# A transformer block on one core: weight splitting moved to the first attention block, key loads by pairs, and a changed planner table

## The chip, the cores and the metric

The kernel runs on one core of a Trainium2 chip. The metric is the device time of one execution in microseconds (us), from its start to its end; smaller is better. The core has five engines that run their own instruction streams in order: TensorE (PE, matrix products; PEld is its weight load), VectorE (DVE), ScalarE (ACT), GpSimd (POOL) and SyncE (SP), which here does nothing but issue DMAs. An instruction that waits holds back everything behind it on its engine.

## The reference

One block: an adaptive layer norm, multi-head attention with 32 heads of width 18 on 2048 tokens of width 576, a second adaptive layer norm, and a two-layer network of width 4608 with SiLU.

```python
mod = (_silu(c) @ w_mod).reshape(c.shape[0], 6, 1, -1)
sa, ca, ga, sb, cb, gb = (mod[:, 0], ..., mod[:, 5])
h = _layernorm(x, axis=-1) * (1 + ca) + sa
x = x + ga * _A_ref(h, A_wqkv, A_wo)     # softmax(q k^T / sqrt(18)) v, then @ wo
h = _layernorm(x, axis=-1) * (1 + cb) + sb
x = x + gb * _B_ref(h, B_w1, B_w2)       # silu(h @ w1) @ w2
```

## The kernel before

**Number format.** To keep precision with TensorE's reduced fp32 format, weights and activations are split into a high and a low part and multiplied in three products (high-high, high-low, low-high). Splitting a weight means a load into `raw`, a copy with rounding on POOL (`CAST`, high part), a subtraction on POOL (low part) and, since the same weights are needed four times, a store of both parts to a scratch tensor (`w1s`, `w2s`, `wos`). The function `weights` does this for the first of the four uses; later uses load the two parts from scratch.

**Staging.** The first part (to about 150 us) makes the first layer norm, the first q, k and v projections and their splits, and starts the scores. Then the attention runs in 4 query blocks of 512 tokens. A block has 8 "quads" of 4 heads, a quad 32 "slots", a slot two score pairs. For each pair TensorE makes two products at once, each on half of its rows: `psa` (scores, `ka` times `qt`, whose maximum DVE takes, `slot_a`) and, 40 slots later in the program (`LEAD`), `psb` (the same scores transposed, `kb` times `qt`, with the maximum subtracted inside the product; ACT takes the exponential into a `pt` buffer, `slot_b`). Then `psv` multiplies `pt` with the values (`pv`, four column groups of the array at once). When a quad is done, ACT copies `psv` to `ov`, DVE transposes and normalises it, and SP copies the heads into `ou` by DMA (`out_b`).

**Filler work.** Between score pairs TensorE is given other work from a list (`Filler`). In block 0 this is the rest of the q/k projections (`psqk`, function `qk_one`, weights by `qk_load`). When that list is empty, `open_mlp` closes the memory pools of the projections and opens the pool `mlp` in their place. In block b+1 the filler is what follows the attention of block b: splitting `ou` into `th` and `tl` (`o_T`), the output projection (`psp`), layer norm, transposes (`h_T`), and the network (`mlp1`, `mlp2`, with the weights `w1t` and `w2t`). The network of the last block runs alone at the end.

**What sets the order.** TensorE's order is written by a planner (`Plan`): a clock with costs in ns for each kind of work, queues for ACT and DVE with a duration for each operation (`TMAX` for a maximum, `TEXP` for an exponential), and rings for the PSUM banks, so that a product is put where its bank should be free. It is a list made at build time; on the chip only semaphores decide when things run. The other engines' orders (ACT, DVE, POOL and SP) come from a list scheduler with a timeline of its own, which may pull an instruction ahead of others if its inputs look ready.

**Lines that the steps touch.** `L690` psa, `L692` its maximum, `L739` psb, `L741` its exponential, `L776` psv, `L780` the copy to ov, `L804` ou from ov, `L872` the copy th from ou, `L664` key loads, `L717` and `L721` the maxima's way through DRAM (mscr) into the rows of `qt`, `L834` raw loads, `L837` and `L838` the split on POOL, `L839` the store of a split weight, `L565` and `L572` ACT's copies of a finished projection, `L588` its store, `L900` the addition of an output to x on POOL.

## Time and profile before

| | |
|---|---|
| median of 3 runs | 2464.64 us (2460.85 to 2469.64) |
| the profiled execution | 2463.14 us, of which 2461.4 us are the span from its first to its last instruction |
| busy in the span | PE 96%, DVE 73%, ACT 61%, POOL 26% |
| granted TensorE clock, mean | 0.981 |
| DMA | 433.01 MB, 176 GB/s in the mean |

Busy times of PE are modelled ends of pipelined products, so 96% does not mean that it works at its peak. A row of the timeline gives start, duration, engine, line, operation, output and inputs, and in brackets how long the engine was idle before and what released it. Rows of the windows view give a stretch in us, then its length, then per engine the busy time and the instruction count in the order PE, PEld, DVE, ACT, POOL, then the granted clock, the share of the 16 DMA engines and GB/s.

### The profile page before, as it was taken

Reading aid. Unit: us, or ns where it says so; the run is one execution under the profiler, and the core shown is the slowest. Engines: PE = TensorE matmul, PEld = TensorE weight load, DVE = VectorE, ACT = ScalarE, POOL = GpSimd, SP = SyncE. Lnnn points to the kernel's source line nnn. Section 1 sums busy time; section 2 is a strip of 40 time slices with the busy share of each in tenths; the row PEclk is TensorE's granted clock in tenths of the full one; section 3 lists DMA queues with packets and bytes.
Section 4 is the critical chain, followed back from the end, with each engine's and each line's share of the span. In section 5 each row is a group of like instructions: output and inputs, shape, how many; then the busy total and the mean of one; then the engine's idle time right before and its main releaser. Section 6 shows DMA issues by size and latency. Waiting matters only on the chain.

```text
span 2461.4 us, 52349 instructions
## 1 busy us (share of the span) xinstructions
PE 2359.8 (96%) x19952; PEld 1585.1 (64%) x19952; DVE 1789.9 (73%) x3110; ACT 1497.0 (61%) x2736; POOL 628.6 (26%) x763
## 2 busy tenths in 40 slices
PE   6989999998999999999999999998999999989999
PEld 4864444433556666766667667775666766678998
DVE  7868888876777888777888888887888788234333
ACT  4227777765566777666677677775677677732121
POOL 5201111122565666554211111112211111110000
PEclk9999999999899999999999999999999999999999
DMA  7744445454466676664545554453655454426563
GB/s 242 250 154 151 147 150 161 143 160 146 144 202 195 227 227 209 206 211 164 182 147 202 171 178 157 164 179 117 217 176 162 155 197 165 133 90 241 183 214 119
DMA packets 201458, 433.01 MB, mean 176 GB/s; under 512 B 31354, under 2 KB 67610, under 8 KB 201210
## 3 DMA queue, kind: packets, MB, share of 16 engines
q1 hardware_dynamic: 196618, 427.37, 52.4%
q8 instruction: 160, 2.62, 0.5%
q10 hardware_dynamic: 4592, 2.29, 0.4%
q14 instruction: 88, 0.72, 0.1%
HBM read 338.53 MB, written 86.33 MB: 173 GB/s over the span
## 4 chain that ended last, share of the span: by engine, by line
PE 82%; DMA 6%; DVE 5%; POOL 2%; ACT 2%; issue 2%; SPq 1%; ACTq 0%; POOLq 0%; DVEq 0%
PE ps L480 25%; PE psv L776 17%; PE psa L690 12%; PE ps L474 10%; PE psb L739 8%; PE psqk L561 4%; DVE mx L692 2%; PE psv L480 2%; PE psp L480 1%; DMA raw<-in_w 1%; DMA mscr<-mt 1%; PE psv L1238 1%; PE psqk L1238 1%; PE psqk L480 1%; PE psp L474 1%
## 5 line engine op out<-in xcount | busy, mean ns | idle before, releaser
L692 DVE TENSOR_REDUCE mx<-psa 128x1 f32<-128x512 f32 x2048 | 1333.0, 684 | 334.5 <-PE psb L739 199.6
L741 ACT ACTIVATE pt<-psb 128x512 f32<-128x512 f32 x2048 | 1150.5, 598 | 511.0 <-PE psb L739 350.0
L739 PE MATMUL psb<-qt,kb 56*128 56x512 f32 x2048 | 772.6, 427 | 39.2 <-ACT pt L741 22.0
L690 PE MATMUL psa<-ka,qt 54*128 54x512 f32 x2016 | 739.4, 420 | 10.9 <-DVE mx L692 8.7
L690 PEld LDWEIGHTS psa<-ka,qt 54*128 54x128 f32 x2016 | 344.1, 188 | 316.3 <-DVE mx L692 213.4
L776 PE MATMUL psv<-pt,vt 128*32 128x512 f32 x4096 | 521.4, 608 | 2.0 <-ACT ov L780 2.0
L480 PE MATMUL ps<-w2t,g 64*128 64x288 f32 x4992 | 418.4, 296 | 0.2
L739 PEld LDWEIGHTS psb<-qt,kb 56*128 56x128 f32 x2048 | 357.4, 187 | 90.3 <-ACT pt L741 61.0
L480 PEld LDWEIGHTS ps<-w2t,g 64*128 64x128 f32 x4992 | 390.7, 188 | 32.7 <-DVE mx L692 13.4
L480 PE MATMUL ps<-hh,w1t 64*128 64x512 f32 x2160 | 384.7, 395 | 1.7 <-DVE x L896 1.6
L480 PEld LDWEIGHTS ps<-hh,w1t 64*128 64x128 f32 x2160 | 216.4, 186 | 60.6 <-DVE mx L692 10.9
L1016 POOL TENSOR_TENSOR g<-etmp,g 128x512 fp32r<-128x512 f32 x108 | 138.8, 1305 | 397.6 <-ACT g L1015 318.0
L776 PEld LDWEIGHTS psv<-pt,vt 128*32 128x32 f32 x4096 | 98.5, 109 | 211.7 <-issue 203.4
L900 POOL TENSOR_TENSOR x<-x,gt 128x288 f32<-128x288 f32 x116 | 92.7, 801 | 427.0 <-ACT gt L899 426.9
L480 PE MATMUL ps<-hl,w1t 64*128 64x512 f32 x864 | 181.1, 392 | 0.0
L896 DVE TENSOR_TENSOR x<-ps,x 128x288 f32<-128x288 f32 x184 | 83.8, 456 | 122.0 <-PE ps L474 76.6
L474 PE MATMUL ps<-w2t,g 128*128 128x288 f32 x960 | 132.9, 299 | 7.4 <-ACT g L1015 5.9
L474 PEld LDWEIGHTS ps<-w2t,g 128*128 128x128 f32 x960 | 130.6, 191 | 9.9 <-ACT g L1015 6.3
L1012 ACT ACTIVATE eq<-ps 128x512 f32<-128x512 f32 x36 | 21.5, 598 | 146.4 <-PE ps L474 146.4
L474 PE MATMUL ps<-hh,w1t 128*128 128x512 f32 x360 | 106.9, 390 | 0.5 <-DVE hh L415 0.5
L480 PEld LDWEIGHTS ps<-hl,w1t 64*128 64x128 f32 x864 | 90.5, 187 | 16.5
L1013 DVE SCALAR_TENSOR_TENSOR etmp<-etmp 128x512 f32<-128x512 f32 x108 | 78.1, 759 | 22.1 <-ACT etmp L1012 21.3
(141 smaller groups left out, 2025.4 us busy)
## 6 DMA issues: line engine op xcount, KB each, us to landing
w1t<-w1s SPq DMA_DIRECT2D x108, 640.0 KB
w2t<-w2s SPq DMA_DIRECT2D x108, 576.0 KB
kb<-kscr SPq DMA_DIRECT2D x512, 108.0 KB
ka<-kscr SPq DMA_DIRECT2D x504, 108.0 KB
w1s<-w1t SPq DMA_DIRECT2D x36, 640.0 KB
w2s<-w2t SPq DMA_DIRECT2D x36, 576.0 KB
vt<-vscr SPq DMA_DIRECT2D x32, 608.0 KB
qt<-qscr SPq DMA_DIRECT2D x128, 108.0 KB
```

Source lines behind the costliest of these rows:

```text
L474: mm(self.ps[late], lhsT=lhsT, rhs=rhs, start=(i == 0), stop=(i == self.n - 1))
L480: done = mm(self.ps[g], lhsT=lhsT[rows], rhs=rhs[rows], start=(s == 0), stop=(s == 2 * self.n - 1))
L561: mm(qk_ps[0], lhsT=w[b][:, kt, :], rhs=(hTl if a else hTh)[:, kt, n * 512:(n + 1) * 512], start=(i == 0), stop=(i == 13))
L690: mm(ps, lhsT=t["q"][64 * j:64 * j + 54, hp, stt * P:(stt + 1) * P], rhs=t["a" if ("a", kc, hp) in t else "b", kc, hp][64 * j:64 * j + 54, ...
L692: return lambda: nc.vector.tensor_reduce(t["mx"][:, 2 * j + hp, stt, kc:kc + 1], ps, axis=AX.X, op=ALU.max)
L739: mm(ps, lhsT=t["b", kt // 4, hp][64 * e:64 * e + 56, kt % 4 * P:(kt % 4 + 1) * P], rhs=t["q"][64 * e:64 * e + 56, hp, :], start=True, sto ...
L741: nc.scalar.activation(t["P"][kt, hp][:, e, :], ps, AF.Exp, scale=SCALE)
L776: mm(t["ps"][32 * h:32 * h + 32, :], lhsT=t["v"][:, c0:c0 + 32], rhs=t["P"][kt, h // 2][:, h % 2, :], start=(kt == 0), stop=(kt == NKT - 1 ...
L896: nc.vector.tensor_add(c["x1"][j][:, hs], ps, c["x1"][j][:, hs])
L900: nc.gpsimd.tensor_add(c["x1"][j][:, hs], c["x1"][j][:, hs], t)
L1013: nc.vector.scalar_tensor_tensor(t, t, 1.0, u, op0=ALU.add, op1=ALU.mult)
L1016: (nc.vector if last else nc.gpsimd).tensor_tensor(g[:, 1, :], t, f(g[:, 0, :]), op=ALU.subtract)
```

## The change

- The first-layer weights (36 tiles) and the output weights (5) are split during block 0's projections, in a staging pool `early` (tiles `we`, 2 buffers; `raw`, 3 buffers), and stored to scratch. Block 0's own network then loads them from scratch. The second-layer weights are still split where they were.
- Key loads are asked for one pair of heads at a time, at four points of every 8 slots: slot 1 (second pair of the next `ka`), slot 5 (first pair of the one after), slots 2 and 4 (the two pairs of the next `kb`). Before, all four loads of a ring were asked for at slot 0.
- The copies `th` from `ou` get a dependency on the score product that TensorE's order has last at that point (`after_pe`).
- The q/k weights are loaded over SP instead of ACT's queue, and the load is asked for earlier than the split.
- `pt` has 7 buffers until `open_mlp` and 10 from then on (3 are taken from the `mlp` pool, and are the next to be used); the planner's durations are shorter (`TMAX` 690 to 605, `TEXP` 600 to 495) with a latency added behind each operation (`TLAT`); `LP`, a pause that the filler's pace counts ahead of block 0's transposes, goes from 8000 to 2000.

```diff
-LP = 8000
-PB = 10
+LP = 2000
+PB = 7, 10
-TMAX, TEXP = 690, 600
+TMAX, TEXP = 605, 495
+TLAT = {"A": 100, "V": 85}
...
-                done(s + dur)
+                done(s + dur + TLAT[e])
...
+    def after_pe(ins):
+        if state["pe"] is not None:
+            tc.add_manual_dep(ins.ins, state["pe"].ins.name, SYNC, reason="its turn by the plan")
...
     def qk_load(which, m, i):
-        raw = qk_raw.pop(i)() if i in qk_raw else raw_load(qk_src(which, m), KT * P, nc.scalar)
+        if i not in qk_raw:
+            raw = raw_load(qk_src(which, m), KT * P, nc.sync)
+            qk_raw[i] = lambda: raw
+
+    def qk_split(i):
+        raw = qk_raw.pop(i)()
         hi = hi_part(raw)
...
                     if n == pairs[0][0] and p == 0 and i + 1 < len(steps):
                         load(i + 1)
+                    if n == pairs[0][1] and p == 0 and i + 1 < len(steps):
+                        split(i + 1)
+                    if p % 2 == 1 and splits:
+                        fill.add(0, splits.pop(0))
...
+    def early(src, scr, gate=None):
+        weights(mp["e"].tile([P, 2, 640], F32R, tag="w", name="we", bufs=2)[:, :, :src.shape[1]], src, scr, True, gate)
...
+    splits = [lambda i=i: early(w1[i], w1s[i]) for i in range(NFT)] + [lambda kt=kt: early(wo[:, kt, :], wos[kt], ga) for kt in range(KT)]
...
-        if (s + KLD) % 8 == 0 and 32 <= s + KLD < 32 * NQ:
-            load_k("a", (s + KLD) // 8)
+        n, w = divmod(s, 8)
+        if w == 1:
+            if s == LEAD + 1:
+                load_k("a", n + 1, 0)
+            load_k("a", n + 1, 1)
+        elif w == 5:
+            load_k("a", n + 2, 0)
...
-            if s % 8 == 0 and s and s + 8 < 32 * NQ:
-                load_k("b", s // 8 + 1)
+            if s >= 8 and s % 8 in (2, 4):
+                load_k("b", s // 8 + 1, s % 8 // 2 - 1)
...
-            t["P"][kt, hp] = pts[s % PB]
+            t["P"][kt, hp] = pts[0]
+            pts.append(pts.pop(0))
...
+        pts[:0] = [mp["p"].tile([P, 2, QB], F32, name=f"pt{i}") for i in range(*PB)]
...
-            weights(w, wo[:, kt, :], wos[kt], b == 0, ga)
+            weights(w, None, wos[kt], False)
...
-            nc.scalar.activation(hi[:n], src[:n], AF.Copy)
+            after_pe(nc.scalar.activation(hi[:n], src[:n], AF.Copy))
...
-            weights(c["w1", i], w1[i], w1s[i], b == 0)
+            weights(c["w1", i], None, w1s[i], False)
```

**How the orders move.** Three places matter below. The first is ACT at the end of block 0's projections. The last projection is copied out (`qkhl`, `qt`), then exponentials (`pt`) follow. Before:

```order
L572 ACTIVATE qkhl<-psqk 128x512 [waits DMAHW6_49,DMAHW5_49,PE_49]
L565 ACTIVATE qt<-psqk 128x512 [waits Pool_49]
L741 ACTIVATE pt_2089<-psb 128x512 [waits PE_49]
L741 ACTIVATE pt_2090<-psb 128x512 [waits PE_49] x2
L741 ACTIVATE pt_2091<-psb 128x512 [waits PE_49] x2
L872 ACTIVATE th<-ou 128x512 [waits DMAHW2_49,DMAHW4_49,DMAHW1_49,DMAHW6_49,DMAHW0_49,Pool_49]
```

After, at the same place (`pt_6971` is the first of the three buffers in the `mlp` pool):

```order
L580 ACTIVATE qkhl<-psqk 128x512 [waits DMAHW4_49,DMAHW0_49,PE_49]
L573 ACTIVATE qt<-psqk 128x512 [waits Pool_49]
L779 ACTIVATE pt_6971<-psb 128x512 [waits DMAHW2_49,DMAHW6_49,DMAHW0_49,DMAHW7_49,PE_49,Pool_49]
L779 ACTIVATE pt_6971<-psb 128x512 [waits PE_49]
L779 ACTIVATE pt_6972<-psb 128x512 [waits PE_49] x2
```

The first three copies `th` have left this place. The wait for POOL and for DMAs, which goes with the first tile that is written in the new pool (its memory was that of the projections' tiles, whose last stores have to land), now stands on an exponential, directly behind the projection's copies.

The second place is ACT at the end of a block's last quad, where `ov` is copied and the last two copies `th` wait for its way through DVE and the DMAs `ou<-ov`. Here the end of block 0, before:

```order
L780 ACTIVATE ov<-psv_6339 128x512
L741 ACTIVATE pt_2096<-psb 128x512 x2
L741 ACTIVATE pt_2097<-psb 128x512 x2
L872 ACTIVATE th<-ou 128x512
L741 ACTIVATE pt_2098<-psb 128x512 x2
L741 ACTIVATE pt_2089<-psb 128x512
L872 ACTIVATE th<-ou 64x512
```

After:

```order
L818 ACTIVATE ov<-psv_6772 128x512
L779 ACTIVATE pt_2098<-psb 128x512 x2
L896 ACTIVATE th<-ou 128x512 x3
L779 ACTIVATE pt_2092<-psb 128x512 x2
L779 ACTIVATE pt_6971<-psb 128x512 x2
L779 ACTIVATE pt_6972<-psb 128x512 x2
L779 ACTIVATE pt_6973<-psb 128x512 x2
L779 ACTIVATE pt_2093<-psb 128x512 x2
L896 ACTIVATE th<-ou 128x512
L896 ACTIVATE th<-ou 64x512
```

Between `ov` and the copy that needs it stand 12 exponentials and three other copies, where 4 exponentials stood. At the ends of blocks 1 and 2 there are 12 exponentials now where 6 and 2 stood.

The third place is SP in block 0's second quad. Before, a stretch of it:

```order
L664 DMA ka_80<-kscr 54x512 x2
L664 DMA kb_86<-kscr 54x512 x2
L664 DMA ka_81<-kscr 54x512 x2
L664 DMA kb_87<-kscr 54x512 x2
L586 DMA kscr<-qkhl 128x512
L588 DMA kscr<-qkhl 128x2x512
```

After, a stretch with the same key loads:

```order
L696 DMA ka_80<-kscr 54x512
L649 DMA w1s<-we 128x1280
L696 DMA ka_80<-kscr 54x512
L644 DMA raw<-in_w 128x320 x2
L649 DMA w1s<-we 128x1280
L644 DMA raw<-in_w 128x320 x2
L649 DMA w1s<-we 128x1280
L644 DMA raw<-in_w 128x320
L696 DMA kb_86<-kscr 54x512 x2
```

The scheduler does not spread the 36 first-layer splits over block 0's projections: of their stores 16 stand between the first and the second DMA `mscr<-mt` (one per quad), 15 between the second and the third, 5 between the third and the fourth, and none later. DMAs on SP in these three intervals are 92, 98 and 66, where they were 40, 52 and 51.

Counted over the whole order, TensorE changes between its three kinds of work (products on half of the rows, on the full array, and by column groups for the values) 908 times before and 857 times after: 449 and 431 times in block 0, 38 and 29 in the first quad of block 1. In that quad it now has 72 half-row products of the first layer where it had 36.

77 lines of the change are left out of this document (38 added, 39 removed).

## The prediction

> **What bounds the kernel now.** I read the page's first part, then the windows by stage: first attention block (154 to 514 us), the turn to block 1 (to 600), block 1 to its last quad (to 1062), two stretches of eight quads (to 1580 and 2098), and the network alone.
>
> ```profile
> PE 2359.8 (96%) x19952; PEld 1585.1 (64%) x19952; DVE 1789.9 (73%) x3110; ACT 1497.0 (61%) x2736; POOL 628.6 (26%) x763
> 154.00:514.00 360.00, 357.83 (x2207) 156.00 (x2204) 301.40 (x512) 262.50 (x508) 38.90 (x31) 1.00 0.47 148
> 514.00:600.00 86.00, 71.32 (x373) 27.62 (x371) 59.40 (x101) 52.50 (x98) 26.70 (x36) 0.89 0.56 178
> 600.00:1062.00 462.00, 444.13 (x4118) 299.94 (x4115) 360.77 (x605) 303.89 (x551) 277.45 (x384) 0.97 0.60 196
> 1062.00:1580.00 518.00, 507.45 (x4891) 348.63 (x4890) 411.92 (x698) 357.43 (x649) 123.66 (x140) 0.99 0.53 177
> 1580.00:2098.00 518.00, 508.47 (x4955) 349.70 (x4954) 416.12 (x708) 359.74 (x655) 91.29 (x91) 0.99 0.50 167
> ```
>
> TensorE is the bound. It is full in the first window (357.8 of 360) and idles by 15 us in the second and 18 in the third, against 10 to 11 in the later two; there, too, the clock is lowest and POOL busiest. From 514 to 1062 are 548 us for eight quads that later take 518: that is where something can be won. So I looked in the timeline at what ended TensorE's idle times of more than 1 us. Most are ACT's waits at the copies `th`:
>
> ```profile
>   DMA ou<-ov: 14.5, 4
>   DMA qscr<-qkhl: 4.3, 1
> 543.52 1.15 ACT L872 ACTIVATE th<-ou 128x512 fp32r<-128x512 f32 x2 [4.35 <-DMA qscr<-qkhl]
> 545.21 0.79 PE L739 MATMUL psb<-qt,kb 56*128 56x512 f32 x1 [4.78 <-ACT pt L741]
> 596.32 0.63 ACT L872 ACTIVATE th<-ou 128x512 fp32r<-128x512 f32 x1 [5.65 <-DMA ou<-ov]
> 597.49 1.28 PE L739 MATMUL psb<-qt,kb 56*128 56x512 f32 x2 [5.03 <-DMA ka<-kscr]
> 1151.77 0.63 ACT L872 ACTIVATE th<-ou 128x512 fp32r<-128x512 f32 x1 [3.47 <-DMA ou<-ov]
> 1674.87 0.63 ACT L872 ACTIVATE th<-ou 128x512 fp32r<-128x512 f32 x1 [4.27 <-DMA ou<-ov]
> 595.00:602.00 7.00, 4.51 (x16) 1.80 (x16) 1.99 (x3) 3.77 (x8) 1.27 (x1) 0.51 0.17 53
> 1151.00:1158.00 7.00, 5.07 (x25) 2.87 (x27) 2.33 (x4) 3.79 (x7) 1.27 (x1) 0.53 0.29 93
> 1677.00:1684.00 7.00, 5.64 (x29) 3.02 (x29) 3.86 (x6) 3.76 (x7) 0.00 (x0) 0.51 0.03 12
> ```
>
> ACT stands at a copy, exponentials queue behind it, banks stay taken, `psb` stops. Each stop is followed by about 7 us at half the clock.
>
> **The change part by part.** The sum is made against the profiled execution, 2463.1 us; the median of the runs is 1.5 us above it. A difference under 0.3% (7.4 us) is what a measurement here cannot tell from none.
>
> *Copies in TensorE's order.* At the block ends they now stand behind 12 exponentials, where they stood behind 4, 6 and 2. At 0.8 to 0.95 us an exponential (a quad's 64 in 51 to 62 us) these and the three other copies take over 11 us; `ov` to `th` took 8 to 9 (in the timeline around the rows above). So the 14.5 us of waits should go: **+13**, 12 to 14.5. The three slow-clock stretches cost up to 3.5 us each, but part of that time is idle anyway: **+6**, 0 to 10.
>
> *The first wait stays.* At 543.52 the copy waited for the projections' last store. By the order that wait now stands on the first exponential in a new buffer, and no exponential is ahead of it.
>
> ```profile
> 535.44 0.59 ACT L565 ACTIVATE qt<-psqk 128x512 f32<-128x512 f32 x1
> 536.11 1.28 POOL L566 TENSOR_TENSOR qkhl<-qt,qkhl 128x512 fp32r<-128x512 f32 x1 [11.97 <-ACT qt L565]
> 537.41 0.39 SPq L588 DMA_DIRECT2D qscr<-qkhl  x1
> ```
>
> From the end of `qt` (536.0) to the release (543.5) are 7.5 us, in which before five exponentials ran. ACT stands 7.5 instead of 4.35: **-3**, -5 to 0. This part of the stall moves and does not go.
>
> *First-layer splits out of block 1.* They leave POOL 98 us lighter there, of 277.
>
> ```profile
> L838 POOL TENSOR_TENSOR w1t<-raw,w1t 128x320 fp32r<-128x320 f32 x72 | 63.4, 892 | 0.3
> L837 POOL CAST w1t<-raw 128x320 fp32r<-128x320 f32 x72 | 34.4, 487 | 74.4 <-DMA raw<-in_w 45.6 <-DMA kb<-kscr 9.1 <-PE psa L690 7.5
>   DMA raw<-in_w: 121.5, 77
> 638.30 0.46 DVE L906 BATCH_NORM_STATS2 st<-x 128x6 f32<-128x288 f32 x1 [4.47 <-POOL x L900]
> 639.85 0.79 PE L690 MATMUL psa<-ka,qt 54*128 54x512 f32 x1 [2.77 <-DVE mx L692]
> 641.00:657.00 16.00, 15.12 (x54) 6.57 (x53) 11.54 (x24) 8.75 (x15) 10.89 (x15) 0.52 0.69 235
> ```
>
> What POOL's time costs is its order: it stood 121.5 us at loads not yet landed, with the additions to x behind. At 638 that stopped DVE, then TensorE for 2.8 us, and 16 us at half clock followed, worth up to 8. Second-layer splits stay and keep some such waits: **+12**, 3 to 16.
>
> *The burst.* The order puts 31 of the 36 splits into two quads of block 0.
>
> ```profile
> L717 SPq DMA_DIRECT2D mscr<-mt x32: 342/343/1072, 153.9 to 2098.0; - x32
> 258.83 0.34 SPq L717 DMA_DIRECT2D mscr<-mt  x1
> w1s<-w1t SPq DMA_DIRECT2D x36, 640.0 KB
> raw<-in_w SPq DMA_DIRECT2D x72, 160.0 KB
> 200.00:250.00 50.00, 50.00 (x304) 21.54 (x296) 41.63 (x71) 36.84 (x71) 5.37 (x4) 1.00 0.46 148
> 2220.00:2230.00 10.00, 7.10 (x39) 4.94 (x38) 7.08 (x14) 3.64 (x5) 2.93 (x4) 1.00 1.01 401
> 80.00:100.00 20.00, 20.00 (x192) 17.38 (x193) 16.72 (x37) 2.66 (x7) 1.54 (x1) 1.00 1.01 316
> ```
>
> These quads last from 153.9 to 258.8, 104.9 us. POOL has room: 31 x 2 x (0.487 + 0.892) = 85.5 us. The DMA engines have less: a split moves 640 + 2 x 160 KB = 0.98 MB, 31 of them 30.5 MB; at 148 GB/s the quads' own traffic is 15.5 MB; 46.0 MB in 104.9 us are 439 GB/s. With all engines busy (share 1.01) the trace shows 401 and 316. SP issues in order, so key loads stand behind loads and stores that wait, and fall behind with them. At 401 GB/s the two quads take 114.7 us, at 316 145.6, which is 10 or 41 late. What hides a delay is the key loads' lead: a `kb` load for a pair is now asked for 5 or 6 slots ahead (8 and 9 before), 8 to 10 us; a store of 512 KB landed 6 us after its issue (537.4 to 543.5), a key load is smaller. I take 4 us as cover: a loss of 6 to 37. The splits' packets are large like those of the 401 row, so I stay in the lower half: **-15**. The Trainium skill, "DMA: Bandwidth & Descriptors" (Specifications), gives about 358 GB/s as one core's share of HBM and 435 as the fabric's ceiling; by the first the loss would be about 20 and the sum 5 us worse, by the second about none. The 401 row speaks against the first as a hard limit.
>
> *Fewer changes of kind on TensorE.* Counted over the order, 51 fewer.
>
> ```profile
> 580.44 0.50 PE L739 MATMUL psb<-qt,kb 56*128 56x512 f32 x1
> 581.87 0.50 PE L690 MATMUL psa<-ka,qt 54*128 54x512 f32 x1
> 582.21 0.39 PE L690 MATMUL psa<-ka,qt 54*128 54x512 f32 x1
> 582.44 0.39 PE L690 MATMUL psa<-ka,qt 54*128 54x512 f32 x1
> 670.68 1.93 PE L776 MATMUL psv<-pt,vt 128*32 128x512 f32 x16
> 672.53 0.50 PE L690 MATMUL psa<-ka,qt 54*128 54x512 f32 x1
> ```
>
> Two value tiles take 1.85 us (670.68 to 672.53), one 0.93. From the `psb` at 580.44 over one value tile to the `psa` at 581.87 are 1.43 us; less the tile and a product's 0.23 (582.21 to 582.44), 0.27 remain, and 0.11 more before the next `psa` (0.34 for 0.23). A pair of changes costs 0.27 to 0.38, 51 changes 7 to 10. Some fall in the burst: **+8**, 5 to 10.
>
> *Earlier network work.* 36 more half-row products in block 1's first quad, where TensorE had idle time, at half of 0.23 us each: **+4**, 0 to 8. With `LP` gone the transposes `h_T` come a few slots behind the last `psp`, and their layer norm may not be ready: **-2**, -4 to 0, once.
>
> *Key loads by pairs.* Both rings' loads keep their number. The waits `psb` had for `qt<-mscr` may shrink when SP is blocked less; a shorter `kb` lead may add some:
>
> ```profile
>   PE psb L739: 9.7, 4
> ```
>
> **+1**, -4 to +10.
>
> *At nothing.* The q/k weights' 7 loads on SP are asked for one step ahead, and a step of two units is some 30 us in this stage. 7 `pt` buffers: the order has as many runs of value products in block 0 (127) as before, so the cover is the planner's own check. Shorter planner durations cost nothing by themselves; what they do is in the order above.
>
> Sum: 13 + 6 - 3 + 12 - 15 + 8 + 4 - 2 + 1 = **24 us faster**, 2439; with the median's 1.5 us, **2440.5**.
>
> **The rivals.** *The burst starves the scores* (slower). Without its term the sum is 39 faster. It cancels that when the two quads are 43 us late, 148 us, that is at 311 GB/s; below 296 the kernel is slower by more than the bound. At 270 GB/s they take 170 us, 61 lost: 2463 - 39 + 61 = 2485, 2487 as a median. For it: mixed loads and stores have no row above 316 that lasts 20 us, and a core that waits keeps its clock low. Against: the two rows quoted, and that POOL's and SP's waits also make the demand drop.
>
> *The waits move.* The copies' 19 us come back as the longer first wait, as waits of `h_T`, and as ACT's three copies in a row; 24 - 19 = 5 faster, 2459 (2460). For it: the first wait moved just so. Against: 12 exponentials are more than the trace's 8 to 9 us.
>
> *The burst costs nothing and block 1 becomes like the others*: 548 against 518 us is 30, with the copies at blocks 1 and 2 and the order 47: 2416 (2418).
>
> **How the numbers follow.** Forecast 0.62, between 2418 and 2456; the waits move 0.12; the starved scores 0.20; the larger gain 0.06. Range 2412 to 2474: from the terms' good ends, a little beyond the larger gain, into the lower part of the starved case, leaving out its worse half (0.1) and a tenth for the rest. Faster by over 0.3%: 0.62 + 0.06 = 0.68; the waits move is the same, 0.12; slower 0.20.
>
> **What would show it.** Right: `th` no longer waits for `ou<-ov` before 2100; one exponential waits about 7.5 us for `qscr<-qkhl` near 540; POOL busy about 180 in block 1's eight quads instead of 277, and no half-clock stretch of 16 us near 640; DMA share near 1 from 155 to 260 with the third `mscr<-mt` later than 258.8 by some 15 us. Wrong: the third `mscr<-mt` later by over 40 us, with `ka` and `kb` loads ending TensorE's waits there; or not later at all, and then the time is near 2425; or waits of exponentials behind `th` as long as before.

## The result, and the profile after

| | median, us | ratio to the kernel before (95% interval) |
|---|---|---|
| before | 2464.56 (2460.85 to 2469.64, 4 runs) | |
| changed | 2493.38 (2491.18 to 2497.5, 4 runs) | 1.0117 (1.0095 to 1.014) |

The kernel is 29 us slower; 24 us faster was forecast, and the range ended at 2474. All windows, waits and intervals below come from the one profiled execution of each kernel; times and ratios are of all its runs. The windows by stage of the changed kernel say where (columns as before: PE, PEld, DVE, ACT, POOL busy, granted clock, DMA share, GB/s):

```profile
154.00:206.00 52.00, 40.76 (x218) 16.69 (x218) 35.00 (x57) 28.05 (x54) 27.30 (x44) 0.91 0.81 263
206.00:259.00 53.00, 33.35 (x142) 13.97 (x142) 19.98 (x33) 18.43 (x34) 31.30 (x48) 0.70 0.79 264
259.00:312.00 53.00, 41.06 (x205) 18.04 (x203) 26.29 (x45) 24.04 (x46) 26.69 (x39) 0.81 0.82 279
312.00:365.00 53.00, 40.88 (x225) 16.64 (x225) 33.30 (x53) 28.33 (x54) 19.65 (x26) 0.87 0.77 251
365.00:514.00 149.00, 148.29 (x901) 62.76 (x903) 128.12 (x221) 113.48 (x223) 38.37 (x44) 1.00 0.58 178
577.00:1097.00 520.00, 496.27 (x4401) 328.54 (x4401) 406.61 (x690) 345.23 (x640) 200.32 (x257) 0.96 0.55 181
```

Block 0's first quads, where TensorE was full before, are now its emptiest place: 156 of 211 us, at a clock of 0.70 to 0.91. From 365 us on TensorE is full again. The DMA engines are busy, but at 0.77 to 0.82 and not at 1.

One mark makes the kernels comparable: the DMA `mscr<-mt`, issued once a quad when its maxima are complete. Its start times on SP are numbered from 0 here, and the intervals are differences of these times, in us:

| | transfer 0 at | 0 to 1 | 1 to 2 | 2 to 3 | three together | 8 to 15 |
|---|---|---|---|---|---|---|
| before | 153.9 | 53.3 | 51.6 | 49.4 | 154.3 | 484.3 |
| changed | 144.4 | 90.5 | 85.6 | 55.5 | 231.5 | 455.9 |

So 9.6 us are won ahead of the first transfer, 77 lost in three intervals, and 28 won back in block 1; the other 11 are won in small parts, 4 in intervals 3 to 8 and 7 behind transfer 15. The largest single stop is in SP's order. Timeline rows of the changed kernel, SP first, then TensorE:

```profile
222.09 3.35 SPq L644 DMA_DIRECT2D raw<-in_w  x2
225.93 0.33 SPq L649 DMA_DIRECT2D w1s<-we  x1
226.34 0.38 SPq L644 DMA_DIRECT2D raw<-in_w  x1
226.82 0.32 SPq L696 DMA_DIRECT2D kb<-kscr  x1
227.19 0.95 SPq L594 DMA_DIRECT2D kscr<-qkhl  x1
...
231.97 0.54 SPq L596 DMA_DIRECT2D kscr<-qkhl  x1
...
234.84 0.38 SPq L754 DMA_DIRECT2D mscr<-mt  x1
239.15 1.28 SPq L758 DMA_DIRECT2D qt<-mscr  x2
224.12 0.50 PE L727 MATMUL psa<-ka,qt 54*128 54x512 f32 x1
242.03 0.89 PE L777 MATMUL psb<-qt,kb 56*128 56x512 f32 x2 [17.41 <-DMA qt<-mscr]
```

TensorE has finished the quad's last `psa` at 224.6, and DVE its last maximum at 225.4. The maxima leave only at 234.84, because raw loads, split stores and projection stores stand ahead of them on SP, and TensorE stands until 242. What SP waited for from 154 to 365 us (waits of the DMA queue; total, times, longest):

```profile
SPq L644 <- POOL we L648: 31.2, 20, 2.6
SPq L644 <- DMA raw<-in_w: 10.7, 9, 2.7
SPq L649 <- POOL we L648: 9.0, 16, 2.0
```

Raw loads wait until POOL's subtraction has freed one of three buffers (20 times), stores until that subtraction is done (16 times): 40 us of waits for POOL, with the key loads and the maxima behind.

### The profile page after: what moved, and what is told of

Its sections match the earlier page's. It is cut to its first block, busy times and chain, and to the rows that moved or that the text cites. A ratio compares the mean times of both kernels' runs of the same rounds, so it can differ in the third digit from the quotient of the medians.

```text
span 2489.4 us, 52376 instructions
## 1 busy us (share of the span) xinstructions
PE 2357.8 (95%) x19952; PEld 1615.3 (65%) x19952; DVE 1781.6 (72%) x3110; ACT 1482.3 (60%) x2736; POOL 627.6 (25%) x763
## 2 busy tenths in 40 slices
DMA packets 208003, 459.56 MB, mean 185 GB/s; under 512 B 32010, under 2 KB 68266, under 8 KB 207754
## 4 chain that ended last, share of the span: by engine, by line
PE 82%; DMA 6%; DVE 5%; ACT 3%; POOL 2%; issue 2%; SPq 1%; ACTq 0%; POOLq 0%; DVEq 0%
PE ps L483 25%; PE psv L814 17%; PE psa L727 12%; PE ps L477 10%; PE psb L777 9%; PE psqk L569 3%; DMA raw<-in_w 3%; DVE mx L729 2%; PE psv L483 2%; PE psp L483 1%; DMA kb<-kscr 1%; PE psv L1262 1%; PE psqk L483 1%; ACT pt L779 1%; PE psqk L1262 1%
## 5 line engine op out<-in xcount | busy, mean ns | idle before, releaser
L779 ACT ACTIVATE pt<-psb 128x512 f32<-128x512 f32 x2048 | 1131.4, 598 | 554.2 <-PE psb L777 372.0
L777 PE MATMUL psb<-qt,kb 56*128 56x512 f32 x2048 | 762.3, 432 | 71.5 <-ACT pt L779 22.2
L727 PE MATMUL psa<-ka,qt 54*128 54x512 f32 x2016 | 703.8, 421 | 10.3 <-DVE mx L729 8.8
L777 PEld LDWEIGHTS psb<-qt,kb 56*128 56x128 f32 x2048 | 357.1, 188 | 122.2 <-ACT pt L779 57.5
L483 PE MATMUL ps<-w2t,g 64*128 64x288 f32 x4992 | 408.5, 293 | 0.2
L483 PEld LDWEIGHTS ps<-w2t,g 64*128 64x128 f32 x4992 | 382.6, 186 | 30.7 <-DVE mx L729 7.5
L483 PE MATMUL ps<-hh,w1t 64*128 64x512 f32 x2160 | 397.9, 393 | 2.5 <-DVE x L920 1.5
L483 PEld LDWEIGHTS ps<-hh,w1t 64*128 64x128 f32 x2160 | 247.3, 185 | 37.9 <-DVE mx L729 7.5
L483 PE MATMUL ps<-hl,w1t 64*128 64x512 f32 x864 | 200.2, 391 | 0.0
L483 PEld LDWEIGHTS ps<-hl,w1t 64*128 64x128 f32 x864 | 107.3, 186 | 9.3
```

The source lines that it names most:

```text
L483: done = mm(self.ps[g], lhsT=lhsT[rows], rhs=rhs[rows], start=(s == 0), stop=(s == 2 * self.n - 1))
L727: mm(ps, lhsT=t["q"][64 * j:64 * j + 54, hp, stt * P:(stt + 1) * P], rhs=t["a" if ("a", kc, hp) in t else "b", kc, hp][64 * j:64 * j + 54, ...
L777: state["pe"] = mm(ps, lhsT=t["b", kt // 4, hp][64 * e:64 * e + 56, kt % 4 * P:(kt % 4 + 1) * P], rhs=t["q"][64 * e:64 * e + 56, hp, :], s ...
L779: nc.scalar.activation(t["P"][kt, hp][:, e, :], ps, AF.Exp, scale=SCALE)
```

## The experiments

**Which part costs, which part gains.**

*Splits' DMAs on POOL's queue* (`weights`, while the early pool is open):

```diff
-            nc.sync.dma_start(raw, src[:, cs])
+            q.dma_start(raw, src[:, cs])      # q = nc.gpsimd for the early splits
-        nc.sync.dma_start(f(scr), f(w))
+        q.dma_start(f(scr), f(w))
```

> The changed kernel with one edit: the early splits' loads and stores are issued from POOL's own queue and no longer from SP's; their bytes, their tiles and their place in POOL's order stay. The changed kernel is at 2493 us and loses 73 us against the kernel before between the first and the eighth transfer of the maxima (231.5 us for the first three intervals instead of 154.3). Theory 'queue' (each split's loads wait on SP until POOL has freed one of three buffers, and the key loads stand behind them): nothing of the splits stands in SP's order any more, the three intervals fall to 155 to 175 us, the time to 2420 to 2440. Theory 'bandwidth' (30 MB more than the DMA engines can move beside the key loads): the same bytes in the same stretch, so the three intervals stay over 210 us and the time over 2475. In between (some of each) it would be 2440 to 2475.

Measured: 2484.8 us, ratio 1.0086 (1.0062 to 1.011); intervals 82.1, 75.2, 54.1, together 211.3. Neither theory's number: 20 of the 77 us come back in these intervals, 9 in all. The splits now take longer: of their 36 first-layer stores 10, 10 and 6 start in the three intervals, where the changed kernel has all 36 (16, 15, 5), and 10 later. So the bytes did not stay in the same stretch, as the theory of bandwidth had it, and the first interval is 82.1 us long at only 195 GB/s. The waits say why. SP now stands once, for 27 us, at the projection's store `kscr<-qkhl`, which waits for POOL's subtraction `qkhl`, and POOL is still in the splits:

```profile
SPq L596 <- POOL qkhl L574: 36.0, 2, 27.0
223.81 0.39 SPq L596 DMA_DIRECT2D kscr<-qkhl  x1
224.71 0.53 SPq L755 DMA_DIRECT2D mscr<-mt  x1
PE psb L778 <- DMA qt<-mscr: 35.7, 2, 31.1
```

The link broke and the next one held: POOL's order in place of SP's.

*Six staging buffers* for the early raw loads:

```diff
-            raw = mp.get("p", mp.get("e")).tile([P, 320], F32, tag="raw", name="raw", bufs=3)[:, :n]
+            raw = mp.get("p", mp.get("e")).tile([P, 320], F32, tag="raw", name="raw", bufs=(3 if "p" in mp else 6))[:, :n]
```

> The changed kernel with six staging buffers for the early raw loads instead of three. Theory 'queue': a split now takes a round trip of load, POOL and release, 5.7 us on average in the two quads with 31 of them, where POOL alone needs 2.76 us; with twice the buffers SP waits for POOL less, and 20 to 50 of the 73 us come back: 2445 to 2475. Theory 'bandwidth': loads are asked for earlier, nothing moves faster: 2488 to 2500, the three intervals near 231 us.

Measured: 2482.6 us, ratio 1.0073 (1.0053 to 1.0093); intervals 84.5, 85.6, 51.9, together 222.0. 11 us come back, fewer than the queue theory wanted, more than none. The edit did not do what that theory asked of it: SP's waits for POOL stay at 40 us (34.0 at loads, 6.3 at stores). From 154 to 312 us the engines are busier instead, at 0.86 to 0.88 and 286 to 299 GB/s. So this run does not separate the two theories.

*Spread* (each early raw load depends on TensorE's last score product):

```diff
-            nc.sync.dma_start(raw, src[:, cs])
+            ld = nc.sync.dma_start(raw, src[:, cs])
+            if "p" not in mp:
+                after_pe(ld)
```

> The changed kernel with one edit: each early raw load also waits for the score product that TensorE's order has last at that point, so that the splits keep the places which the filler list gives them (by the order 4, 8, 5, 7, 6, 6 of the first-layer splits in the first six quads of block 0 instead of 16, 15, 5). Both theories, queue and bandwidth, expect most of the 73 us back, since the rate falls to a third: 2420 to 2440, below the kernel before at 2464.6. A third view, that a split in block 0 costs its time wherever it stands (its key loads are late by a POOL round trip each time): 41 x 2 us or so stay, 2455 to 2490.

Measured: 2462.9 us, ratio 0.9988 (0.9973 to 1.0004). The three intervals fall to 181.2, but the next ones rise to 60.6, 59.2 and 56.3. The third view came true: spread, a split still costs in block 0. POOL waits longer now, for loads that wait for TensorE, and what else stands on POOL and SP waits with it:

```profile
POOL we L649 <- DMA raw<-in_w: 201.3, 46, 12.9
```

*The split undone*:

```diff
-    splits = [...]
+    splits = []
-            weights(w, None, wos[kt], False)
+            weights(w, wo[:, kt, :], wos[kt], b == 0, ga)
-            weights(c["w1", i], None, w1s[i], False)
+            weights(c["w1", i], w1[i], w1s[i], b == 0)
```

> The changed kernel without the moved splits: first-layer and output weights are split in block 1 as before, everything else stays as changed. The 73 us of block 0 go in every theory. If POOL's relief in block 1 was worth the +12 us of the prediction: 2493 - 73 + 12 = 2432 us. If the 28 us that the changed kernel wins back between the ninth and the sixteenth transfer of the maxima come from the splits' absence alone: 2493 - 73 + 28 = 2448. If that gain is due to the copies and the order: 2420 to 2425.

Measured: 2438.6 us, ratio 0.9898 (0.9879 to 0.9917). Transfer 0 at 146.2; intervals 52.4, 58.3, 49.1, together 159.8; 8 to 15 takes 480.9. So without the moved splits the change is 26 us faster, and all of the loss is theirs: 231.5 against 159.8 us in block 0, of which they give back 25 in block 1 (455.9 against 480.9; by medians 71.7 - 54.8 = 17). The time lies between the first two numbers foreseen, 2432 and 2448.

**The other parts.** Each is undone on this kernel (2438.6 us).

*Copies free again*:

```diff
-            after_pe(nc.scalar.activation(hi[:n], src[:n], AF.Copy))
+            nc.scalar.activation(hi[:n], src[:n], AF.Copy)
```

> The kernel with the split undone (2438.6 us), with one more edit: the copies th no longer wait for TensorE's order, so that the scheduler may pull them ahead as in the kernel before. The prediction's terms for them, 13 + 6 us: 2457.6, 2450 to 2463. Rival 'the waits move' (the copies' gain comes back at once as other waits): 2438 to 2446.

Measured: 2462.3 us, ratio 0.999 (0.9977 to 1.0003): 23.7 us, 19 foreseen. The waits `th` for `ou<-ov` are back, 18.4 us in all, where the changed kernel has one of 4.0:

```profile
ACT th L896 <- DMA ou<-ov: 18.4, 5, 11.0
```

*q/k weights on ACT's queue again*, asked for at the split:

```diff
-            raw = raw_load(qk_src(which, m), KT * P, nc.sync)
...
-        raw = qk_raw.pop(i)()
+        raw = qk_raw.pop(i)() if i in qk_raw else raw_load(qk_src(*steps[i][:2]), KT * P, nc.scalar)
```

> The kernel with the split undone (2438.6 us), with the q/k weights loaded over ACT's queue at the split again, as before the change. The kernel before has one idle time of TensorE of 6.2 us at 129 us, ended by an issue on ACT's queue, and the changed kernels have none and are 8 to 11 us ahead at the first transfer of the maxima. If that came from the loads on ACT's queue: 2438.6 + 9 = 2448, with the first transfer of the maxima near 154 us. If not (the prediction costed this part at nothing): 2436 to 2442, near 146.

Measured: 2451.0 us, ratio 0.9945 (0.9932 to 0.9958): 12.4 us, and transfer 0 at 154.1, 7.9 us later; where the rest of the 12.4 lies stays open. The row of the kernel before that I had passed over is in TensorE's timeline (`ACTq L491` is a marker in ACT's order; just ahead of it, at 128.40, ACT issues a load of q/k weights):

```profile
129.07 0.85 PE L480 MATMUL psv<-wv,hTh 64*128 64x288 f32 x4 [6.18 <-ACTq L491]
```

*The planner's numbers of before*:

```diff
-LP = 2000
+LP = 8000
-TMAX, TEXP = 605, 495
-TLAT = {"A": 100, "V": 85}
+TMAX, TEXP = 690, 600
+TLAT = {"A": 0, "V": 0}
```

> The kernel with the split undone (2438.6 us), with the planner's numbers of before (longer durations, no latency behind them, the longer pause ahead of block 0's transposes). By the prediction's terms for them (+8 fewer changes of kind, +4 earlier network work, -2 for the transposes' wait) it is 10 us slower: 2449, 2444 to 2455. Rival: the kernel with the split undone, less the measured copies (23.7 us) and q/k weights (12.4 us), would stand at 2474.7, 9 us above the kernel before, so the rest of the change costs something, and if that is the planner's numbers, this kernel is 5 to 10 us faster: 2429 to 2434.

Measured: 2433.9 us, ratio 0.9876 (0.9851 to 0.9902), against 0.9898: not told apart, and not 10 us slower; its median is within the rival's range. The interval 1 to 2 is 51.6 again instead of 58.3; later intervals give that back.

*Old key loads*:

```diff
-        n, w = divmod(s, 8)
...
+        if s % 8 == 0:
+            for hp in range(2):
+                load_k("a", s // 8 + 1, hp)
...
-            if s >= 8 and s % 8 in (2, 4):
-                load_k("b", s // 8 + 1, s % 8 // 2 - 1)
+            if s % 8 == 0 and s:
+                for hp_ in range(2):
+                    load_k("b", s // 8 + 1, hp_)
```

> The kernel with the split undone (2438.6 us), with all four key loads of a ring asked for at once at every eighth slot, as before. By the prediction (+1, from -4 to +10) it is 1 us slower, 2435 to 2449. Rival (the rest of the change costs 9 us, and it is the shorter lead of the key loads): 2429 to 2434.

Measured: 2442.0 us, ratio 0.99 (0.9877 to 0.9923), against 0.9898: no difference.

**Bytes or order.** These kernels follow the links one by one, or add one cost alone to the kernel with the split undone.

*Projections' stores on POOL's queue too* (in `qk_store`):

```diff
+        q = nc.gpsimd if "t" in qk_ps else nc.sync
-                nc.sync.dma_start(f(dst[:, 2 - 2 * a]), f(hl[p0:p1, 0]))
+                q.dma_start(f(dst[:, 2 - 2 * a]), f(hl[p0:p1, 0]))
-                nc.sync.dma_start(f(dst[:, a:a + 2]), f(hl[p0:p1]))
+                q.dma_start(f(dst[:, a:a + 2]), f(hl[p0:p1]))
```

> As the kernel with the splits' DMAs on POOL's queue (2484.8 us; there SP stood from 196.8 to 223.8 us at the store of a projection, which waits for POOL's subtraction of that projection, which stood in POOL's order behind splits that waited for their loads). Now the projections' stores in block 0 go over POOL's queue as well, behind that subtraction, so that SP never waits for POOL there. All splits' bytes and their places on POOL stay. Theory 'chain' (POOL in order behind the splits, SP in order behind POOL, key loads behind SP): the first three intervals of the maxima's transfers fall from 211 to 155-170 us and the time to 2420-2440. Theory 'bandwidth' (the extra 30 MB): the intervals stay over 200 us, the time over 2470.

Measured: 2474.0 us, ratio 1.003 (1.0017 to 1.0042); intervals 52.3, 103.3, 54.1, together 209.7. The first interval is whole again: SP no longer waits for POOL there. But POOL, with one queue more in its order, also thins the burst out: 5 of the splits' first-layer stores start in this interval, then 13 and 7, so fewer bytes go through it as well. The second interval, at 220 GB/s, holds new stops, again by POOL's order. SP, which was to wait for POOL no more, stands 50.0 us at a load of q/k weights that waits for POOL's `wql`. ACT's copy `qt` waits for a buffer that POOL's subtraction frees, 19.5 us, with the exponentials behind it:

```profile
260.33 0.60 ACT L573 ACTIVATE qt<-psqk 128x512 f32<-128x512 f32 x1 [19.47 <-POOL qkhl L574]
259.02 1.28 POOL L574 TENSOR_TENSOR qkhl<-qt,qkhl 128x512 fp32r<-128x512 f32 x1
```

*Spread, and off SP*: the edits of the spread, of the splits' DMAs and of the projections' stores together.

```diff
+            ld = q.dma_start(raw, src[:, cs])
+            if "p" not in mp:
+                after_pe(ld)
```

> Splits spread over block 0 by TensorE's order, their DMAs and the projections' stores on POOL's queue: SP has the key loads and waits for POOL nowhere in block 0. Theory 'chain': block 0 costs what it does without the splits, and block 1 keeps the 25 us that it gains without them (between the ninth and the sixteenth transfer of the maxima the changed kernel gains 28.4 us on the kernel before, the kernel with the split undone 3.4): 2438.6 - 25 = 2414, range 2408 to 2425. Theory that each split costs time wherever it stands (bytes, or POOL beside DVE): 2440 to 2463, like the spread kernel at 2463.

Measured: 2439.8 us, ratio 0.9904 (0.9885 to 0.9924); intervals 52.1, 71.2, 49.6; 8 to 15 takes 453.8. The time is at the edge of the second theory's range. Block 1 keeps its gain, block 0 still loses: SP stands 20.8 us at one load of q/k weights that waits for POOL's `wql`. But two windows bear on the bytes (here the splits' go over POOL's queue):

```profile
SPq L532 <- POOL wql L542: 20.8, 1, 20.8
259.00:312.00 53.00, 53.00 (x327) 21.93 (x325) 46.33 (x79) 40.62 (x80) 34.68 (x54) 1.00 0.79 264
312.00:365.00 53.00, 52.63 (x314) 22.52 (x312) 44.48 (x77) 40.00 (x78) 36.80 (x56) 1.00 0.81 268
```

At the rate and the DMA share of the changed kernel's burst, TensorE is full and at full clock. POOL is busier there, 34.7 and 36.8 of 53 us, than anywhere in that burst (31.3 at most), and DVE is at 0.84 to 0.87, so POOL's arithmetic beside DVE is not what stops TensorE.

*That load on POOL's queue too*:

```diff
-            raw = raw_load(qk_src(which, m), KT * P, nc.sync)
+            raw = raw_load(qk_src(which, m), KT * P, nc.gpsimd)
```

> As the kernel with the spread splits off SP (2439.8 us; its second interval took 71.2 us instead of about 52, and there SP stood 20.8 us at the load of the next q/k weights, which waits for POOL's subtraction wql of the weights before). Now that load goes over POOL's queue too, so that in block 0 SP waits for nothing of POOL. Theory 'chain': the second interval falls to 50-56 us and the time by 12 to 20, to 2420-2428. Theory that the splits cost their time in another way (bytes, POOL beside DVE): the interval stays over 62 us, 2434 to 2442. The clock then stays at 1.00 there and the DMA engines near 260 GB/s in both.

Measured: 2435.7 us, ratio 0.988 (0.9858 to 0.9901); intervals 52.3, 61.7, 57.5, together 171.5. The second interval improves by 10, less than 'chain' expected, and the time is in the other theory's range. In the second interval SP still stood 10.6 us, until 251.2, at a query load whose store now stands on POOL's queue. The third loses 8: there TensorE waits 7.9 us for the maxima, whose two DMAs are 7.8 us apart.

```profile
SPq L690 <- DMA qscr<-qkhl: 10.6, 1, 10.6
PE psb L781 <- DMA qt<-mscr: 7.9, 1, 7.9
```

*POOL's work alone*:

```diff
+        if j == 0 and s < 62 and s % 2 == 0:
+            for cs in (slice(0, 320), slice(320, 640)):
+                ins = nc.gpsimd.tensor_copy(wed[:, 1, cs], rawd)
+                if cs.start == 0:
+                    after_pe(ins)
+                nc.gpsimd.tensor_tensor(wed[:, 0, cs], rawd, f(wed[:, 1, cs]), op=ALU.subtract)
```

> The kernel with the split undone (2438.6 us), with POOL's work of 31 splits added in the first two quads' scores, every second slot in TensorE's order: 31 times two roundings and two subtractions of 128x320 on a tile filled once, with no DMA. POOL beside DVE (or POOL's time as such) as the cause: 85 us of POOL work make the first three intervals over 180 us instead of 159.8. Theory 'chain' (POOL's work costs when it waits for loads): 158 to 165 us, and 2436 to 2444.

Measured: 2446.3 us, ratio 0.9919 (0.9902 to 0.9935); three intervals 158.6. But only the first rounding of each split waited for TensorE, and half of the work ran ahead of transfer 0: POOL is busy 54.4 us in the three intervals, against 14.8 without the added work. So 40 us of added arithmetic cost nothing there; this run says nothing of 85. (The two windows of the spread kernel off SP above, with POOL busier, are the better evidence.) The time is 7.6 us above the base's and over the range of 'chain'; these intervals do not explain that, and its cause stays open.

*Bytes added, first form*, from DRAM to DRAM:

```diff
+        if j == 0 and s < 62 and s % 2 == 0:
+            after_pe(nc.gpsimd.dma_start(dscr[s // 2][:, :640], w1[s // 2]))
+            nc.gpsimd.dma_start(dscr[s // 2][:, 640:], w1[s // 2][:, :320])
```

> The kernel with the split undone (2438.6 us; the intervals of the maxima's transfers 0 to 1, 1 to 2 and 2 to 3 are 52.4, 58.3 and 49.1 us, 159.8 together), with 31 pairs of DMAs added in the first two quads' scores, every second slot: each pair copies 480 KB of the first layer's weights from DRAM to a scratch tensor that nothing reads, 0.98 MB moved, as much as a split moves. They are issued from POOL's queue in TensorE's order, go to no buffer that has to come free, and POOL computes nothing for them. Bytes as the prediction costed them: the two quads are late by 10 to 41 us, the three intervals 170 to 200 us, the time 2448 to 2480. Theory 'chain' (the bytes cost little, the waits of SP for POOL and of POOL for loads cost it all): 158 to 167 us and 2436 to 2446.

Measured: 2451.1 us, ratio 0.9935 (0.9917 to 0.9954); three intervals 157.2. This seems to acquit the bytes, but only the first copy of each pair waited for TensorE; the other 31, of 160 KB each, ran before 140 us. *Doubled*:

```diff
-            nc.gpsimd.dma_start(dscr[s // 2][:, 640:], w1[s // 2][:, :320])
+            for c0 in (640, 1280):
+                nc.gpsimd.dma_start(dscr[s // 2][:, c0:c0 + 640], w1[s // 2])
```

> As the kernel with the bytes alone (2451.1 us, three intervals of 49.8, 57.9 and 49.5 us), with twice the bytes per pair: 960 KB copied from DRAM to DRAM for each of the 31, so that the DMA engines, which count such a copy once, have as much to move as for a split, and DRAM twice as much. Theory 'chain': the three intervals stay under 170 us, the time 2445 to 2458. Bytes: near 439 GB/s wanted for the two quads against 401 seen at most, so they stretch by 10 to 41 us, three intervals of 168 to 200 us, 2458 to 2490.

Measured: 2492.1 us, ratio 1.011 (1.0078 to 1.0142), with the three intervals at 162.1 and transfer 0 at 190.1 instead of 146.2: 63 of the 93 copies ran before 140 us. The run is no test of the two quads, but it shows what full engines do to the first part, 44 us:

```profile
20.00:40.00 20.00, 3.58 (x12) 2.33 (x12) 5.62 (x20) 4.76 (x7) 11.14 (x17) 1.00 1.01 379
60.00:80.00 20.00, 6.11 (x20) 4.89 (x20) 3.82 (x15) 1.28 (x2) 13.61 (x21) 0.57 1.02 361
```

*All copies in place*:

```diff
+        n = 2 * (s % 2) + j
+        if s < 62 and n < 3:
+            after_pe(nc.gpsimd.dma_start(dscr[s // 2][:, 640 * n:640 * n + 640], w1[s // 2]))
```

> In the two kernels with added copies only the first copy of each pair or triple waited for TensorE; the others ran in the first part of the program (63 of them before 140 us in the second kernel, whose first transfer of the maxima was 44 us late while the DMA engines were at 361 to 379 GB/s). Here each of the 93 copies of 320 KB, 0.96 MB for each of 31 splits, waits for its own score product in the first two quads, on POOL's queue, base: the kernel with the split undone (first transfer at 146 us, three intervals of 52.4, 58.3 and 49.1 us, 159.8 together, 2438.6 us). Theory 'chain': three intervals of 158 to 170 us, 2436 to 2448. Bytes (439 GB/s wanted, 401 seen): 170 to 200 us for the three, 2448 to 2480, with the engines' share near 1.

Measured: 2486.5 us, ratio 1.0084 (1.0056 to 1.0111); intervals 64.9, 82.3, 56.8, together 204.0. *And a split's own traffic*:

```diff
+        if s < 62 and n < 2:
+            after_pe(nc.gpsimd.dma_start(mp["e"].tile([P, 320], F32, name="rawd", bufs=6), w1[s // 2][:, 320 * n:320 * n + 320]))
+        elif s < 62 and n == 2:
+            after_pe(nc.gpsimd.dma_start(dscr[s // 2], wed))
```

> The copies in place delayed the three intervals from 159.8 to 204.0 us, with the DMA engines at 0.92, 0.82 and 0.81 of their time; but a copy from DRAM to DRAM costs DRAM twice what it costs the engines. Here the traffic is a split's own, 31 times in the first two quads on the kernel with the split undone: two loads of 160 KB into one of six staging tiles that nothing reads, and a store of 640 KB to scratch from a tile filled once, each waiting for its score product, on POOL's queue, with no arithmetic and no wait of SP for POOL's splits. If the bytes were the whole loss of the changed kernel: 205 to 235 us for the three intervals, 2485 to 2510. If they are a part: 165 to 205 us, 2445 to 2485. If the cost in the kernel before this one came from DRAM's double load: 158 to 165 us, 2436 to 2446, and the changed kernel's loss is the queues' order alone.

Measured: 2480.3 us, ratio 1.0066 (1.004 to 1.0091); intervals 62.2, 79.4, 55.2, together 196.8. The bytes of 31 splits, when they run at the pace of the two quads from POOL's queue, cost 37 us by themselves. Windows, SP's timeline at the second transfer, and TensorE's waits for key loads:

```profile
154.00:206.00 52.00, 47.21 (x245) 19.64 (x249) 38.25 (x65) 31.14 (x61) 24.57 (x45) 0.85 0.93 337
206.00:259.00 53.00, 42.01 (x228) 18.09 (x220) 29.69 (x49) 27.44 (x52) 21.98 (x36) 0.89 0.84 299
206.42 0.34 SPq L755 DMA_DIRECT2D mscr<-mt  x1
221.08 1.28 SPq L759 DMA_DIRECT2D qt<-mscr  x2
SPq L759 <- DMA mscr<-mt: 21.6, 3, 12.6
PE psb L783 <- DMA kb<-kscr: 9.8, 4, 5.3
```

The 16 KB of `mscr` hold SP up for 12.6 us, and the second DMA is issued 14.7 us after the first. TensorE then waits 9.1 us for it (its largest single wait for a DMA there). In the kernel before the two are 1.4 to 4.7 us apart in the first ten quads and 8.5 at most, in the changed kernel 4.3 (234.84 and 239.15 above). So the bytes act in part through the wait for a small transfer beside large ones, and as much through late key loads (9.8 us in four waits). The Trainium skill, "DMA: Bandwidth & Descriptors" (Latency and other measured facts), gives 2 us as DRAM's latency under high load; this run's 12.6 us of waiting for one transfer, in a window at 299 GB/s, is far more than that.

One thing is not the changed kernel's here: the queue. The profile lists what POOL issues as another queue (q0, software) than what SP issues (q1, hardware), and the packets differ. Over the three intervals, first of the changed kernel (144 to 376 us), then of this one (145 to 347):

```profile
DMA packets 30951, 58.74 MB, mean 253 GB/s; under 512 B 4024, under 2 KB 16910, under 8 KB 30935
DMA packets 22392, 53.36 MB, mean 264 GB/s; under 512 B 4003, under 2 KB 6854, under 8 KB 22377
q0 software_dynamic: 7392, 30.32, 40.2%
```

From SP's queue the splits come in many packets under 2 KB, from POOL's queue in packets of 4 KB in the mean (30.32 MB in 7392). What the same bytes cost from SP's queue with nothing waiting, no run shows.

*Split off POOL's other users* (spread; splits' DMAs on POOL's queue; the low parts of projections and q/k weights subtracted by DVE, stores and weight loads on SP again):

```diff
-            hl, tmp = qk_hi(qk_ps[0]), qk_ps["t"].tile([P, 512], F32, name="qt")
-            nc.scalar.activation(tmp, qk_ps[0], AF.Copy)
-            nc.gpsimd.tensor_tensor(hl[:, 1], tmp, f(hl)[:, 0], op=ALU.subtract)
+            hl = qk_hi(qk_ps[0])
+            qk_lo(hl, qk_ps[0])
```

> Splits spread over block 0 by TensorE's order with their DMAs on POOL's queue (as before), but now the other users of POOL leave it: the low parts of the projections and of the q/k weights are subtracted by DVE, the first straight from the accumulator, and ACT's second copy of a projection goes; the projections' stores and the q/k weights' loads are on SP again. So nothing that TensorE needs in block 0 stands behind a split. Theory 'chain': all eight intervals of block 0 near 50 us (402 us from the first to the ninth transfer would be 424 with the split undone, 440 with everything on POOL's queue), and 2410 to 2425 us. If DVE's extra work (24 x 0.69 us and 6 subtractions more, at 83% busy) takes the place: 2428 to 2440.

Measured: 2427.2 us, ratio 0.9856 (0.9825 to 0.9887), the best median of all, and just between the two ranges foreseen. From transfer 0 to 7 it takes 365.3 us, against 361.0 with the split undone and 432.6 in the changed kernel; all 36 first-layer splits are in there:

```profile
154.00:514.00 360.00, 353.74 (x2096) 148.15 (x2096) 312.33 (x536) 253.69 (x486) 168.13 (x280) 0.98 0.76 250
```

The DMA engines carry 250 GB/s for 360 us and TensorE is busy 353.7 of them. That it is not under 2425 is the turn to block 1, whose first interval (7 to 8) takes 76.4 us instead of 63.1.

**The ladder.** The three intervals side by side, with the splits' first-layer stores that start in them:

| | three intervals, us | stores of splits |
|---|---|---|
| changed | 231.5 | 36 |
| splits' DMAs off SP | 211.3 | 26 |
| projections' stores off SP too | 209.7 | 25 |
| a split's traffic only, without POOL's work and its waits | 196.8 | 31 |
| nothing of the splits | 159.8 | 0 |

Of 71.7 us, the steps down to the traffic alone are 20 + 2 + 13 = 35, the last one 37. This does not divide the loss between order and bytes: the second and third kernel also have fewer bytes in these intervals, and the fourth has larger packets from another queue. That the order is enough by itself for 30 us is shown: the kernel with the splits' DMAs off SP has a first interval of 82.1 us at 195 GB/s (52.4 without the splits), and the one with the projections' stores off SP too has a second interval of 103.3 us at 220 GB/s (58.3 without), both below the 264 and 268 GB/s at which TensorE was full. That bytes are enough for 37 us is shown for POOL's queue. How much each would take with the other absent in the changed kernel's own order stays open.

## Why the prediction was wrong

**The step that failed is the burst**, sized -15 in a range of -6 to -37. It measured -72 in block 0. Two things were wrong in it. The rate: I took the lower half because the splits' packets are as large as those of the row with 401 GB/s. They are not: in the changed kernel's three intervals 16910 of 30951 packets are under 2 KB, and the mean is 1.9 KB (58.74 MB in 30951). Its windows have 251 to 279 GB/s at a DMA share of 0.77 to 0.82; scaled to a share of 1 that is some 330 GB/s, an estimate, near the 316 row and not the 401 one. The traffic alone, with its larger packets, reached 337 and 299 GB/s and cost 37 us, the upper end. The Trainium skill, "DMA: Bandwidth & Descriptors" (Specifications), gives about 358 GB/s as one core's share of DRAM, by which the prediction would have lost 20; the run of the traffic alone lost more than that, though single slices of it moved 402 GB/s. And the order was left out of the price. "SP issues in order, so key loads stand behind loads and stores that wait" stands in the text, but only the bytes were priced; the waits of SP for POOL were even counted in favour ("make the demand drop"). The engines do stay at 0.8 of their time, but because the key loads and the maxima are held too: SP waits 40 us for POOL there, and TensorE's longest stop, 17.4 us, is at the maxima.

**The rival "the burst starves the scores"** was right about place and outcome: 2487 foreseen, 2493 measured, with a chance of 0.20. Its mechanism was only half right, as the engines were not at their limit, and the near hit is in part luck: it set a loss of 61 against a gain of 39, and the runs show 71.7 against 42.9. Its break-even, two quads 43 us late, was passed by 28 (transfers 0 to 2 take 176.1 us, 104.9 before).

**The sum without the burst** was 39 us faster. It came to 42.9: 71.7 - 28.8. But its terms moved:

- *Copies*, 13 + 6 = 19: 23.7. Right, and nearly so in the sign given: before 2100 us no copy was to wait for `ou<-ov`, and one does, 4.0 us until 666.
- *The first wait*, -3: right in kind, smaller in size. It stands on the exponential directly behind `qt`, 5.63 us instead of 4.35 and not 7.5:

```profile
609.57 0.63 ACT L573 ACTIVATE qt<-psqk 128x512 f32<-128x512 f32 x1
615.83 1.08 ACT L779 ACTIVATE pt<-psb 128x512 f32<-128x512 f32 x2 [5.63 <-DMA qscr<-qkhl]
```

- *POOL lighter in block 1*, +12 (3 to 16): 17 to 25. Between transfers 8 and 15 POOL is busy 188 us (641 to 1097 us; the 200 in the last window above begin 64 us earlier), 279 before (578 to 1062): 90 us lighter, 98 foreseen. Of the stop near 640 with its 16 us at half clock there is left, at the same distance from transfer 8, one of 2.3 us at 703 with about 6 us of a lower clock (0.83 and 0.60) around it. The gain was under-sized; that is perhaps because the waits at raw loads were priced at one place only, which no run isolates.
- *q/k weights*, at nothing: 12.4. I looked at what the loads cost on SP and not at what they had cost on ACT: an idle time of 6.2 us with a slow clock behind it (0.79 from 130 to 140 us), in a stretch that I had taken as the same in both kernels.
- *Planner* (switches +8, earlier network +4, `h_T` -2): not seen; the old numbers are as fast or faster. Why 51 changes of kind fewer bring nothing is not shown.
- *Key loads*, +1: none.

These measured parts add up to more than 42.9 (23.7 + 12.4 + 17 to 25, less 1), so some 9 to 17 us are lost elsewhere; the kernel with the split undone already lacks 10 of them. Interval 1 to 2 (58.3 instead of 51.6 us, back with the old planner) is one place; the rest stays open, and each of the times is known to some 5 us only by its interval.

The prediction said what would show it wrong: the third transfer over 40 us late, with key loads ending TensorE's waits. It is 61.6 us late, and from 154 to 365 us the key loads end eight of the waits, but the longest one ends with the maxima:

```profile
PE psb L777 <- DMA qt<-mscr: 17.4, 1, 17.4
PE psb L777 <- DMA kb<-kscr: 16.5, 8, 6.1
```

## What to carry to other kernels

Work that looks like filler for an idle engine has its price in the order of the queues that it shares: ask who else stands behind it on the engine, on the DMA queue and in the ring of buffers, and follow that chain to the bound. Breaking one link of such a chain shows the next; the gain came when the splits were spread and nothing that TensorE needs stood behind one any more. A list that spreads work does not bind the scheduler; a dependency does, and a burst of bytes can hurt through a small transfer that something waits for as much as through the large ones. And look in the trace whether added work ran where it was meant to run: in two kernels here half of it and more had gone ahead.

## What the runs showed that I had not expected

- A DMA of 16 KB held the next one up until 14.7 us after its issue, in a window at 299 GB/s of mostly large transfers; in the kernel before it is 8.5 us at most.
- With the splits from POOL's queue, 250 GB/s for 360 us cost 4 us in seven quads; 337 and 299 GB/s in two quads cost 37.
- The same raw loads (144 and 160 KB) go in packets under 2 KB from SP's queue and in larger ones from POOL's: with all splits moved there, the whole execution has 57770 packets under 2 KB instead of 68266, 128 fewer for each of the 82 loads.
- 40 us of added POOL arithmetic beside a DVE at 0.8 of its time changed three intervals by 1 us (158.6 against 159.8).
